# Linear attention and two MLPs on one core: k and v loaded on 112 partitions plus 16, slopes loaded later, sixteen subtractions moved to GpSimd

## The chip, the core and the metric

The kernel runs on one core of a Trainium2 chip. A core has five engines that run in parallel, each with its own list of instructions in a fixed order: TensorE (PE, matrix products), VectorE (DVE), ScalarE (ACT), GpSimd (POOL) and SyncE (SP, which here only issues transfers). A transfer (DMA) is issued by an engine's queue and carried by 16 DMA engines. Engines wait for each other and for transfers through semaphores; an instruction that waits holds up everything behind it on its engine. The metric is the device time of one execution in microseconds (us); lower is better.

## The reference

```python
def _attn_ref(q, k, v):                    # 8 batches, 8 heads, 576 tokens, 64 wide
    q_s = softmax of q over its 64 columns
    k_s = softmax of k over the 576 tokens (axis=2)
    kv = np.einsum('bhsd,bhse->bhde', k_s, v)
    return np.einsum('bhsd,bhde->bhse', q_s, kv)

x = attention, laid out as 4608 tokens x 512
x = square(relu(x @ moe_w_in)) @ moe_w_out             # MLP 1, 512 -> 2048 -> 512
h = x @ moe2_w_in                                      # MLP 2
out = (max(h, 0) + alpha * min(h, 0)) @ moe2_w_out     # alpha: one slope per hidden column
```

In the reference the softmaxes are written out (maximum, exponential, sum plus 1e-9, division), and all is float32. The weights and alpha reach the kernel as 64-bit floats, whose two words it joins into one float32 itself.

## The kernel before

**Products.** Each float32 factor is held as two fp32r parts, a head (the rounded value) and a rest (value minus head), and each product is three matrix products. For MLP 1's first matrix, `Weights` makes 16 chunks f = 0 to 15, each 128 hidden columns wide: SP loads a chunk of 64-bit words into one of two `raw` buffers (L353), ACT corrects the exponent (a rebias) (L366), DVE joins the words in two integer steps (L346, L347) into one of four `bits` buffers, ACT rounds the head (L386), and DVE subtracts it (`rest`, L389).

**Stages.** The 4608 tokens are nine tiles of 512. In the first stage each tile goes through attention and then through the 16 chunks (one unit of 12 products each, L741, evacuated by ACT in L769 and L772 and stored to DRAM). In tile 0 the first four chunks are made in 16 blocks of three products, in the order of the four x parts (L721: x part 0 with chunks 0 to 3, x part 1 with chunks 0 to 3, and so on). Later stages (MLP 1's second matrix, L781; MLP 2, L865 and L781) use sums of blocks made from tokens and weights; none of their lines is touched.

**Attention.** `sums(i, j)` makes the 64 x 64 matrices of two heads of batch i: loads k (L538), takes a maximum over the five tokens of each partition (L548, DVE), turns it on PE and takes the maximum over partitions (L553, L556, L559), subtracts it (L563, DVE), exponential (L568, ACT), product with v (L575, PE), then kv (L580 to L589). v is loaded in rows (L538 too) and copied by ACT beside columns of ones (`v_place`, L545). There are two buffers for raw k and two for raw v. `rows(i, j)` loads q (L619), softmaxes it (L625 to L645: DVE, POOL, ACT, DVE, POOL), turns it (L649), splits it (L652, L655) and multiplies it with kv (L663 to L665); the result is split into x (L668, L671).

**A load of k or v.** The 576 tokens lie five to a partition: 115 partitions of five tokens by SP's queue, and partition 115 with one token by ACT's queue (L542). 32 loads of k and 32 of v are made that way.

**Order.** All instructions are written out by a planner (`Plan.run`), which knows a cost and a due time for each operation and appends them engine by engine; so numbers in the code (costs, `due`) decide the order that each engine's list has. `due` of the rows of tile t is counted back from the tile's products by `TILE` = 40 us. The framework adds the semaphore waits. Transfers of SP and ACT use eight completion counters in turn (DMAHW0 to DMAHW7), and a transfer waits until the one eight places before it has landed.

Of the kernel before, what the change touches and what calls it, by code (L numbers as in the profile page):

```python
# [75 lines left out]
class Plan:  # L76
# [97 lines left out]
    def run(self, real):  # L174
# [8 lines left out]
        while left:  # L183
            best = None
            for engine, ops in ready.items():
                can = []
                places = {}
                for at, op in ops:
                    start = max(at, clock[engine], locked if op.lock else 0.0)
                    where = []  # L190
                    for b in op.new:
                        k = b.kind
                        if k.line[k.made + sum(1 for w in where if w[0].kind is k)] is not b:
                            break
# [24 lines left out]
            if op.engine == "sp":  # L219
                clock["sp"] = start + ISSUE  # L220
                landed = max(landed, start + 0.5) + op.mb / RATE
                op.end = max(landed, start) + LANDED - 0.5
            else:
                clock[op.engine] = op.end = start + op.cost
                if op.lock:
                    locked = op.end
            for b in op.use:
                b.left -= 1
                b.end = max(b.end, op.end)
                if not b.left:  # L230
# [11 lines left out]
def linear_attention_two_mlps(  # L242
# [20 lines left out]
    T = NT // TOK  # L263
    R = TOK // P
    KR = 5
    KP = -(-S // KR)
    VW = D + 1
    assert S - (KP - 1) * KR == 1

    const = ctx.enter_context(tc.tile_pool(name="const", bufs=1))  # L270
    psum = ctx.enter_context(tc.tile_pool(name="psum", bufs=1, space=PSUM))
# [53 lines left out]
    )  # L325

    def first():
        for kt in K["k"].homes:
            nc.vector.memset(sbuf(KR * 2 * D)(kt)[96:KP], -3.4e38)
        for vt in K["vr"].homes:  # L330
            nc.vector.memset(sbuf(KR * 2 * D)(vt)[96:KP], 0.0)
        for vt in K["v"].homes:
            nc.vector.memset(sbuf(KR * 2 * VW, KP)(vt).rearrange("p (r h w) -> p r h w", r=KR, h=2)[:, :, :, D:VW], 1.0)
        for w in K["kvw"].homes:
            nc.gpsimd.memset(sr[:, w * GRAIN:w * GRAIN + 2 * P].bitcast(F32), 0.0)
        make_identity(nc, ident)
# [39 lines left out]
    class Weights:  # L376


        def __init__(self, kd, w):
            self.bufs, self.done = [], []  # L380
            for f in range(NF):
# [3 lines left out]
                def head(bits=bits, parts=parts):  # L385
                    nc.scalar.copy(parts.ap[:, :BANK], bits.ap)  # L386

                def rest(bits=bits, parts=parts):
                    nc.vector.tensor_tensor(parts.ap[:, BANK:], bits.ap, parts.ap[:, :BANK].bitcast(F32), op=ALU.subtract)  # L389

                o = plan.add(head, "act", 0.62, [o], new=[parts], use=[bits])
                o = plan.add(rest, "dve", 0.7, [o], use=[bits, parts], lock=True)
                self.bufs.append(parts)
                self.done.append(o)

# [129 lines left out]

    def sums(i, j, after):

        kt = buf(K["k"], lambda g: sbuf(KR * 2 * D, KP)(g).rearrange("p (h r d) -> p h r d", h=2, r=KR))
        vr = buf(K["vr"], lambda g: sbuf(KR * 2 * D, KP)(g).rearrange("p (h r d) -> p h r d", h=2, r=KR))
        vt = buf(K["v"], lambda g: sbuf(KR * 2 * VW, KP)(g).rearrange("p (r h w) -> p r h w", r=KR, h=2))  # L530
        km, m, rs = buf(K["km"], sbuf(2 * D, KP)), buf(K["m"], sbuf(1)), buf(K["rs"], sbuf(1))
        ke = buf(K["ke"], sbuf(2 * KR * D, KP))
        kvw = buf(K["kvw"], lambda g: sr[:, g * GRAIN:g * GRAIN + 2 * P].rearrange("p (n m) -> p n m", n=2))
        p1, p2, p3 = bank(K["m1"]), bank(K["m2"]), bank(K["s"])
        h, last = slice(2 * j, 2 * j + 2), S - 1

        def load(to, x):
            nc.sync.dma_start(  # L538
                to.ap[:KP - 1].rearrange("p h r d -> p h (r d)"),
                x[i, h, :last, :].rearrange("h (p r) d -> p h (r d)", r=KR),  # L540
            )
            nc.scalar.dma_start(to.ap[KP - 1:KP, :, 0, :], x[i, h, last, :].unsqueeze(0))  # L542

        def v_place():
            nc.scalar.copy(vt.ap[:, :, :, :D], vr.ap.rearrange("p h r d -> p r h d"))  # L545
# [4 lines left out]
            )  # L550

        def k_max_t():
            nc.tensor.transpose(p1.ap[:, :KP], km.ap, ident[:KP, :KP])  # L553

        def k_max_all():
            nc.vector.tensor_reduce(m.ap, p1.ap[:, :KP], axis=AX.X, op=ALU.max)  # L556

        def k_max_back():
            nc.tensor.transpose(p2.ap[:KP, :P], m.ap.to_broadcast([P, KP]), ident)  # L559

        def k_shift():
# [434 lines left out]
```

## Time and profile before

| what | value |
|---|---|
| median of 3 runs | 1659.41 us (1656.95 to 1662.28) |
| the profiled execution | 1665.62 us, its span 1663.7 us |
| PE busy | 1590.5 us (96%) |
| DVE, ACT, POOL busy | 1231.4 (74%), 964.0 (58%), 254.5 (15%) |
| transfers | 287.20 MB, mean 173 GB/s |

The span runs from the first instruction to the last; the profiled execution's own time has 1.9 us more around it. PE is busy nearly all the time from 62 us to the end, so what the kernel loses lies in the time in which PE waits. A row of a timeline reads: start, duration, engine, line, operation, output <- input, how many, and in brackets the idle time before it with what ended it. "SPq" and "ACTq" are the engines' queues, in which transfers are issued.

### The profile page before, as it was taken

The numbers are of one execution on the slowest core, as the hardware profiler recorded it, in microseconds if no ns is written. First come the engines' busy times: TensorE is split into PE (matmuls) and PEld (weight loads), VectorE is DVE, ScalarE is ACT, GpSimd is POOL, SyncE is SP. The second block draws the span as 40 slices with busy tenths as digits, with TensorE's granted clock in tenths as the row PEclk, the third lists the DMA queues.
The fourth block names the chain that finished last, engine by engine and source line by source line (L and its number), as shares of the span: only waits on it lengthen the run. The fifth ranks groups of instructions, "written<-read, shape, count | busy, mean of one in ns | idle before, by whom it ended". The sixth has DMA issues, their size and how long they took to land.

```text
span 1663.7 us, 30317 instructions
## 1 busy us (share of the span) xinstructions
PE 1590.5 (96%) x11840; PEld 1491.7 (90%) x11840; DVE 1231.4 (74%) x2125; ACT 964.0 (58%) x1499; POOL 254.5 (15%) x228
## 2 busy tenths in 40 slices
PE   2789999999999999999999999999999999999998
PEld 1567888788888999999999999999999899999998
DVE  4775666666643888888878877777776998888875
ACT  2577666676756644444445677777778644444442
POOL 2111111111200000000012333333333000000012
PEclk9999999999999999999999999999999999999999
DMA  4466777778677644444446433333336644444441
GB/s 131 141 213 227 248 264 265 259 280 271 230 259 260 206 140 140 131 130 128 131 138 206 153 129 129 133 124 133 129 127 217 221 146 140 133 128 128 137 136 63
DMA packets 122112, 287.20 MB, mean 173 GB/s; under 512 B 11504, under 2 KB 70256, under 8 KB 121968
## 3 DMA queue, kind: packets, MB, share of 16 engines
q1 hardware_dynamic: 121712, 285.22, 51.4%
q8 instruction: 93, 1.52, 0.4%
q14 instruction: 51, 0.42, 0.1%
q10 hardware_dynamic: 256, 0.03, 0.0%
HBM read 168.83 MB, written 116.39 MB: 171 GB/s over the span
## 4 chain that ended last, share of the span: by engine, by line
PE 71%; DVE 10%; DMA 5%; ACT 4%; issue 3%; POOL 2%; SPq 0%; DVEq 0%; ACTq 0%; POOLq 0%
PE bank L781 41%; PE bank L741 17%; PE bank L865 10%; DVE sr L473 3%; DMA sb<-in_k_dram 1%; POOL sb L930 1%; ACT sb L914 1%; ACT sb L909 1%; DVE sb L894 1%; DMA sb<-in_moe_w_in_dram 1%; DVE sb L900 1%; PE bank L575 1%; DVE sb L489 1%; DMA sb<-in_q_dram 1%; DVE sb L917 1%
## 5 line engine op out<-in xcount | busy, mean ns | idle before, releaser
L781 PE MATMUL bank<-sr 128*128 128x256 f32 x6048 | 730.1, 283 | 5.2 <-DVE sr L473 4.4
L781 PEld LDWEIGHTS bank<-sr 128*128 128x128 f32 x6048 | 727.0, 192 | 8.3 <-DVE sr L473 7.4
L470 ACT CAST sr<-sb 128x512 fp32r<-128x512 f32 (+2 forms) x534 | 366.3, 713 | 383.7 <-PE bank L781 256.1
L473 DVE TENSOR_TENSOR sr<-sb,sr 128x512 fp32r<-128x512 f32 (+2 forms) x534 | 423.3, 817 | 121.7 <-ACT sr L470 121.1
L741 PE MATMUL bank<-sr 128*128 128x512 f32 x1680 | 408.9, 398 | 4.9 <-DVE sr L389 4.9
L741 PEld LDWEIGHTS bank<-sr 128*128 128x128 f32 x1680 | 312.7, 190 | 71.5 <-DVE sr L389 5.9
L865 PE MATMUL bank<-sr 128*128 128x256 f32 x3024 | 367.6, 284 | 8.1 <-DVE sr L473 7.3
L865 PEld LDWEIGHTS bank<-sr 128*128 128x128 f32 x3024 | 365.0, 193 | 10.5 <-DVE sr L473 9.6
L769 ACT ACTIVATE sb<-bank 128x512 f32<-128x512 f32 x144 | 85.7, 596 | 75.9 <-PE bank L741 59.8
L495 POOL TENSOR_TENSOR sb<-sb 128x256 f32<-128x256 f32 x16 | 16.5, 1034 | 735.6 <-DVE sb L489 697.6
L489 DVE TENSOR_TENSOR sb<-sb 128x512 f32<-128x512 f32 x162 | 114.4, 707 | 10.5 <-DMA sb<-y_scratch 10.1
L930 POOL TENSOR_TENSOR sb<-sb 128x1024 f32<-128x1024 f32 x36 | 89.1, 2475 | 154.5 <-ACT sb L929 118.3
L909 ACT ACTIVATE sb<-sb 128x1024 f32<-128x1024 f32 x72 | 76.3, 1059 | 44.9 <-DVE sb L906 44.2
L914 ACT ACTIVATE sb<-sb,al_neg 128x512 f32<-128x512 f32 x144 | 96.4, 716 | 2.3
L772 ACT ACTIVATE sb<-sb 128x512 f32<-128x512 f32 x144 | 90.7, 631 | 4.0 <-DMA r<-sb 0.6
L817 DVE TENSOR_TENSOR sb<-sb,bank 128x512 f32<-128x512 f32 x108 | 71.4, 684 | 21.1 <-PE bank L781 16.7
L645 POOL TENSOR_TENSOR sb<-sb 128x512 f32<-128x512 f32 x36 | 38.8, 1079 | 279.4 <-DVE sb L641 186.7
L495 DVE TENSOR_TENSOR sb<-sb 128x256 f32<-128x256 f32 x146 | 78.0, 539 | 0.5
L894 DVE TENSOR_TENSOR sb<-bank,sb 128x512 f32<-128x512 f32 x72 | 49.3, 684 | 35.8 <-ACT sb L919 23.0
L548 DVE TENSOR_REDUCE sb<-sb 116x128 f32<-116x640 f32 x32 | 41.7, 1302 | 45.0 <-DMA sb<-in_k_dram 30.6
L900 DVE TENSOR_TENSOR sb<-bank,sb 128x512 f32<-128x512 f32 x72 | 49.8, 692 | 28.3 <-PE bank L865 23.3
L903 POOL TENSOR_TENSOR sb<-sb 128x256 f32<-128x256 f32 x72 | 53.2, 740 | 106.7 <-DVE sb L894 77.2
(64 smaller groups left out, 1066.7 us busy)
## 6 DMA issues: line engine op xcount, KB each, us to landing
r<-sb SPq DMA_DIRECT2D x144, 512.0 KB
sb<-r SPq DMA_DIRECT2D x144, 512.0 KB
j<-sb SPq DMA_DIRECT2D x24, 896.0 KB
sb<-j SPq DMA_DIRECT2D x24, 896.0 KB
sb<-in_moe_w_in_dram SPq DMA_DIRECT2D x32, 512.0 KB
sb<-in_moe_w_out_dram SPq DMA_DIRECT2D x32, 512.0 KB
y_scratch<-sb SPq DMA_DIRECT2D x36, 256.0 KB
sb<-y_scratch SPq DMA_DIRECT2D x18, 512.0 KB
```

The source lines that it names most:

```text
L470: nc.scalar.copy(parts.ap[:, :n], what())
L473: nc.vector.tensor_tensor(parts.ap[:, n:], what(), parts.ap[:, :n].bitcast(F32), op=ALU.subtract)
L489: nc.vector.tensor_tensor(two(block(4, 2)), two(block(1, 2)), block(0).unsqueeze(1).to_broadcast([P, 2, HALF]), op=ALU.subtract)
L495: e.tensor_tensor(block(6), block(2), block(4), op=ALU.add)
L741: nc.tensor.matmul(h.ap, w[:, a, c, :], x_parts(x[c][0])[:, b, :], start=(c == 0 and n == 0), stop=(c == KB - 1 and n == 2),)
L769: o = plan.add(lambda: nc.scalar.activation(u.ap, h.ap, AF.Relu), "act", 0.6, [o], new=[u], use=[h])
L772: lambda: nc.scalar.activation(ro.ap[:, half], u.ap, AF.Square), "act", 0.63, [o, even], new=new, use=[u, ro]
L781: nc.tensor.matmul(target[:, m * HALF:(m + 1) * HALF], one[:, u, ms], two[:, w, :], start=start and m == 0 and i == 0, stop=stop and m == ...
L865: nc.tensor.matmul(h.ap[:, m * HALF:(m + 1) * HALF], a[:, u, c * P:(c + 1) * P], b[:, w, :], start=(m == 0 and c == 0 and z == 0), stop=(( ...
L909: nc.scalar.activation(zt.ap, block(0, 4), AF.Relu, scale=-1.0)
L914: nc.scalar.mul(half, half, al_neg[:, f:f + 1])
L930: o = plan.add(lambda: nc.gpsimd.tensor_tensor(block(0, 4), block(0, 4), zt.ap, op=ALU.add), "pool", 2.3, [o], use=[z, zt])
```

## The change

1. **k and v.** 112 partitions hold five tokens, the 16 others one. Both transfers of a load are issued by SP; ACT issues none. All tiles of `sums` now have 128 partitions. The 16 partitions' four unused places keep the values that `first` puts there (very negative for k, zero for v). The planner counts two issues for such a load.
2. **Start.** `first` runs one exponential on a column of `al` before anything else on ACT; the zeros of raw v are set by POOL instead of DVE.
3. **Rests.** The rest of a chunk f < 16, which is all of them, is made by POOL, with 1.4 us in the plan instead of 0.7.
4. **Slopes.** The load of alpha waits for tile 1's first unit, and counts 0.2 MB in the plan instead of 0.05.
5. **Due times.** The rows of tile 1 are due by 30 us per tile instead of 40.

```diff
+AT_START = 16
+TILE1 = 30.0
...
-                clock["sp"] = start + ISSUE
+                clock["sp"] = start + op.cost
...
-    KP = -(-S // KR)
+    KF = (S - P) // (KR - 1)
...
+        nc.vector.memset(al[:, :1], 0.0)
+        nc.scalar.activation(al_neg[:, :1], al[:, :1], AF.Exp)
         for kt in K["k"].homes:
-            nc.vector.memset(sbuf(KR * 2 * D)(kt)[96:KP], -3.4e38)
+            nc.vector.memset(sbuf(KR * 2 * D)(kt)[96:], -3.4e38)
         for vt in K["vr"].homes:
-            nc.vector.memset(sbuf(KR * 2 * D)(vt)[96:KP], 0.0)
+            nc.gpsimd.memset(sbuf(KR * 2 * D)(vt)[96:], 0.0)
...
-                def rest(bits=bits, parts=parts):
-                    nc.vector.tensor_tensor(parts.ap[:, BANK:], bits.ap, parts.ap[:, :BANK].bitcast(F32), op=ALU.subtract)
+                pool = f < AT_START
+
+                def rest(bits=bits, parts=parts, e=nc.gpsimd if pool else nc.vector):
+                    e.tensor_tensor(parts.ap[:, BANK:], bits.ap, parts.ap[:, :BANK].bitcast(F32), op=ALU.subtract)
...
-                o = plan.add(rest, "dve", 0.7, [o], use=[bits, parts], lock=True)
+                o = plan.add(rest, *(("pool", 1.4) if pool else ("dve", 0.7)), [o], use=[bits, parts], lock=True)
...
             nc.sync.dma_start(
-                to.ap[:KP - 1].rearrange("p h r d -> p h (r d)"),
-                x[i, h, :last, :].rearrange("h (p r) d -> p h (r d)", r=KR),
+                to.ap[:KF].rearrange("p h r d -> p h (r d)"),
+                x[i, h, :KF * KR, :].rearrange("h (p r) d -> p h (r d)", r=KR),
             )
-            nc.scalar.dma_start(to.ap[KP - 1:KP, :, 0, :], x[i, h, last, :].unsqueeze(0))
+            nc.sync.dma_start(to.ap[KF:, :, 0, :], x[i, h, KF * KR:, :].rearrange("h p d -> p h d"))
...
-        lk = plan.add(lambda: load(kt, k), "sp", ISSUE, [after], new=[kt], mb=0.295)
+        lk = plan.add(lambda: load(kt, k), "sp", 2 * ISSUE, [after], new=[kt], mb=0.295)
...
-            due = now[0] - TILE * (1 - (j + 1) / KB) - EARLY if t else LEAD + 4 * j
+            due = now[0] - (TILE if t > 1 else TILE1) * (1 - (j + 1) / KB) - EARLY if t else LEAD + 4 * j
...
-    o = plan.add(alphas, "sp", ISSUE, due=60.0, mb=0.05)
+    o = plan.add(alphas, "sp", ISSUE, [h1[1, 0]], due=60.0, mb=0.2)
```

What that does to the order is shown at three places. Line numbers of the changed kernel are four to six higher (L538 and L542 are there L544 and L548, L353 is L357, L389 is L395).

SP's list from the start of the program, before; in brackets the semaphores that an instruction waits for (DVE_49, Pool_49 and so on stand for an engine, DMAHW for the counter of a transfer):

```order
L538 DMA sb<-in_k_dram 115x2x320 [waits DVE_49]
L619 DMA sb<-in_q_dram 128x2x256
L538 DMA sb<-in_k_dram 115x2x320 [waits DVE_49]
L619 DMA sb<-in_q_dram 128x2x256
L538 DMA sb<-in_v_dram 115x2x320 [waits DMAHW0_49,DVE_49]
L538 DMA sb<-in_v_dram 115x2x320 [waits DMAHW1_49,DVE_49]
L353 DMA sb<-in_moe_w_in_dram 128x4x256 [waits DMAHW2_49]
L353 DMA sb<-in_moe_w_in_dram 128x4x256 [waits DMAHW3_49]
L956 DMA al<-in_moe_alpha_dram 128x16x1 [waits DMAHW5_49]
L538 DMA sb<-in_v_dram 115x2x320 [waits DMAHW6_49,DMAHW0_49,Activation_49]
```

The same place of the change:

```order
L544 DMA sb<-in_k_dram 112x2x320 [waits DVE_49]
L548 DMA sb<-in_k_dram 16x2x64
...
L544 DMA sb<-in_v_dram 112x2x320 [waits Pool_49]
L548 DMA sb<-in_v_dram 16x2x64
L544 DMA sb<-in_v_dram 112x2x320 [waits DMAHW0_49,Pool_49]
L548 DMA sb<-in_v_dram 16x2x64 [waits DMAHW1_49]
L357 DMA sb<-in_moe_w_in_dram 128x4x256 [waits DMAHW2_49]
L357 DMA sb<-in_moe_w_in_dram 128x4x256 [waits DMAHW3_49]
L544 DMA sb<-in_v_dram 112x2x320 [waits DMAHW6_49,DMAHW4_49,Activation_49]
```

The first load of v waits for no counter there, the load of alpha is gone from this place, and the third load of v stands right behind the two chunks of weights.

ACT's list from the start, before (L545 copies v, L634 is the exponential of q, L366 the rebias of a chunk, L568 the exponential of k):

```order
L542 DMA sb<-in_k_dram 1x2x64 [waits DVE_49] x2
L542 DMA sb<-in_v_dram 1x2x64 [waits DVE_49] x2
L545 ACT_TABLE_LOAD [waits DMAHW4_49,DMAHW0_49]
L545 COPY sb<-sb 116x10x64 [waits DVE_49]
L542 DMA sb<-in_v_dram 1x2x64 [waits Activation_49]
L545 COPY sb<-sb 116x10x64 [waits DMAHW6_49,DMAHW1_49,DVE_49]
L542 DMA sb<-in_v_dram 1x2x64 [waits DMAHW7_49,Activation_49]
L634 ACTIVATE sb<-sb 128x2x4x64 [waits DMAHW3_49,Pool_49]
L366 ACTIVATE sb<-sb 128x512 [waits DMAHW2_49]
```

And of the change:

```order
L331 ACT_TABLE_LOAD
L331 ACTIVATE al_neg<-al 128x1 [waits DVE_49]
L551 COPY sb<-sb 128x10x64 [waits DMAHW6_49,DMAHW7_49,DVE_49,Pool_49]
L551 COPY sb<-sb 128x10x64 [waits DMAHW0_49,DMAHW1_49,DVE_49,Pool_49]
L640 ACTIVATE sb<-sb 128x2x4x64 [waits DMAHW2_49,Pool_49]
L370 ACTIVATE sb<-sb 128x512 [waits DMAHW2_49]
L574 ACTIVATE sb<-sb 128x640 [waits DVE_49]
```

The table load no longer stands behind a wait for v, and no transfer stands between the computing instructions.

POOL's list of the change, behind its first four operations for q (L637 and L651 subtract the maximum from q and divide it by the sum; L395 is the rest of a chunk):

```order
L637 TENSOR_TENSOR sb<-sb 128x512 x2
L651 TENSOR_TENSOR sb<-sb 128x512
L395 TENSOR_TENSOR sr<-sb,sr 128x512 x2
L651 TENSOR_TENSOR sb<-sb 128x512
L395 TENSOR_TENSOR sr<-sb,sr 128x512 x2
L637 TENSOR_TENSOR sb<-sb 128x512
```

Before, POOL had there only the operations for q, and the rests stood in DVE's list (the second and third of them together, behind the two integer steps of both chunks and behind the sum of q in L639 to L641).

## Rows read from the trace of the kernel before

**Rows 1.** Stretches: us, busy of each engine, PE clock, DMA share, GB/s

```profile
2.90:36.50 33.60, 5.22 (x34) 3.73 (x34) 12.00 (x25) 9.93 (x16) 7.05 (x10) 1.00 0.56 155
36.50:62.80 26.30, 15.45 (x90) 10.36 (x91) 20.98 (x45) 10.34 (x19) 4.80 (x4) 1.00 0.51 144
62.80:126.00 63.20, 55.96 (x317) 44.37 (x316) 47.75 (x94) 46.21 (x85) 9.63 (x8) 0.97 0.58 182
126.00:475.00 349.00, 344.18 (x2008) 281.72 (x2007) 223.14 (x496) 238.89 (x426) 56.13 (x54) 0.99 0.74 256
```

**Rows 2.** Short stretches with transfers of one kind

```profile
34.00:35.00 1.00, 0.00 (x0) 0.00 (x0) 0.00 (x0) 0.15 (x1) 0.00 (x0) 1.00 0.33 124
48.50:50.00 1.50, 1.50 (x3) 0.83 (x3) 1.43 (x4) 1.35 (x2) 0.22 (x1) 1.00 1.09 323
```

**Rows 3.** Timeline of SP's queue, 0 to 40 us

```profile
1.55 0.39 SPq L538 DMA_DIRECT2D sb<-in_k_dram  x1
...
7.45 0.77 SPq L538 DMA_DIRECT2D sb<-in_v_dram  x2
...
10.83 2.05 SPq L956 DMA_DIRECT2D al<-in_moe_alpha_dram  x1
16.70 3.67 SPq L538 DMA_DIRECT2D sb<-in_v_dram  x2
...
27.33 0.26 SPq L538 DMA_DIRECT2D sb<-in_k_dram  x1
...
38.46 0.27 SPq L538 DMA_DIRECT2D sb<-in_k_dram  x1
```

**Rows 4.** Timeline of the computing engines, 0 to 126 us

```profile
7.46 1.23 DVE L548 TENSOR_REDUCE sb<-sb 116x128 f32<-116x640 f32 x1 [3.75 <-DMA sb<-in_k_dram]
14.65 1.28 ACT L545 ACT_TABLE_LOAD   x1 [14.65 <-DMA sb<-in_v_dram]
15.95 0.73 ACT L545 COPY sb<-sb 116x640 f32<-116x640 f32 x1
...
36.47 1.23 DVE L548 TENSOR_REDUCE sb<-sb 116x128 f32<-116x640 f32 x1 [3.40 <-issue]
43.42 1.23 DVE L548 TENSOR_REDUCE sb<-sb 116x128 f32<-116x640 f32 x1 [1.77 <-DMA sb<-in_k_dram]
50.22 2.01 PE L721 MATMUL bank<-sr 128*128 128x512 f32 x3
...
62.80 0.85 PE L721 MATMUL bank<-sr 128*128 128x512 f32 x3
...
123.04 8.23 PE L741 MATMUL bank<-sr 128*128 128x512 f32 x35 [1.58 <-DVE sr L389]
```

**Rows 5.** PE's waits, 0 to 126 us: total, times, longest

```profile
PE bank L721 <- DVE sr L389: 5.4, 1, 5.4
PE bank L741 <- DVE sr L389: 4.9, 4, 2.2
```

**Rows 6.** Lines: L389, and POOL's groups with mean ns

```profile
L389 DVE TENSOR_TENSOR sr<-sb,sr x16: 637/691/1530, 49.5 to 122.3; 128x512 fp32r<-128x512 f32 x16
L903 POOL TENSOR_TENSOR sb<-sb 128x256 f32<-128x256 f32 x72 | 53.2, 740 | 106.7 <-DVE sb L894 77.2 <-DMA y_scratch<-sb 25.6 <-DMA r<-sb 4.0
L930 POOL TENSOR_TENSOR sb<-sb 128x1024 f32<-128x1024 f32 x36 | 89.1, 2475 | 154.5 <-ACT sb L929 118.3 <-DVE sb L489 36.2
L495 POOL TENSOR_TENSOR sb<-sb x16: 732/904/1456, 852.7 to 1639.2; 128x256 f32<-128x256 f32 x16
L542 ACTq DMA_DIRECT2D sb<-in_k_dram x32: 565/566/1192, 1.6 to 417.8; - x32
```

**Rows 7.** Timeline, 93 to 95 us: POOL beside an integer step of DVE

```profile
93.20 1.04 POOL L631 TENSOR_TENSOR sb<-sb 128x512 f32<-128x512 f32 x1
93.55 0.97 DVE L346 TENSOR_SCALAR sb<-sb 128x512 int32<-128x512 int32 x1 [0.62 <-ACT sb L366]
```

**Rows 8.** L346 in all, ns lowest/median/highest

```profile
L346 DVE TENSOR_SCALAR sb<-sb x64: 407/421/972, 41.0 to 500.0; 128x512 int32<-128x512 int32 x64
```

More of the change, by code (lines that the diff above doesn't have):

```diff
@@ L265, in linear_attention_two_mlps @@
     KR = 5
-    KP = -(-S // KR)
+    KF = (S - P) // (KR - 1)
     VW = D + 1
-    assert S - (KP - 1) * KR == 1
+    assert KF * KR + P - KF == S and KF >= 96
     const = ctx.enter_context(tc.tile_pool(name="const", bufs=1))
@@ L327, in first @@
     def first():
+        nc.vector.memset(al[:, :1], 0.0)
+        nc.scalar.activation(al_neg[:, :1], al[:, :1], AF.Exp)
         for kt in K["k"].homes:
-            nc.vector.memset(sbuf(KR * 2 * D)(kt)[96:KP], -3.4e38)
+            nc.vector.memset(sbuf(KR * 2 * D)(kt)[96:], -3.4e38)
         for vt in K["vr"].homes:
-            nc.vector.memset(sbuf(KR * 2 * D)(vt)[96:KP], 0.0)
+            nc.gpsimd.memset(sbuf(KR * 2 * D)(vt)[96:], 0.0)
         for vt in K["v"].homes:
-            nc.vector.memset(sbuf(KR * 2 * VW, KP)(vt).rearrange("p (r h w) -> p r h w", r=KR, h=2)[:, :, :, D:VW], 1.0)
+            nc.vector.memset(sbuf(KR * 2 * VW)(vt).rearrange("p (r h w) -> p r h w", r=KR, h=2)[:, :, :, D:VW], 1.0)
         for w in K["kvw"].homes:
@@ L526, in sums @@
     def sums(i, j, after):
[L528 to L532, printed above, removed]
+        kt = buf(K["k"], lambda g: sbuf(KR * 2 * D)(g).rearrange("p (h r d) -> p h r d", h=2, r=KR))
+        vr = buf(K["vr"], lambda g: sbuf(KR * 2 * D)(g).rearrange("p (h r d) -> p h r d", h=2, r=KR))
+        vt = buf(K["v"], lambda g: sbuf(KR * 2 * VW)(g).rearrange("p (r h w) -> p r h w", r=KR, h=2))
+        km, m, rs = buf(K["km"], sbuf(2 * D)), buf(K["m"], sbuf(1)), buf(K["rs"], sbuf(1))
+        ke = buf(K["ke"], sbuf(2 * KR * D))
         kvw = buf(K["kvw"], lambda g: sr[:, g * GRAIN:g * GRAIN + 2 * P].rearrange("p (n m) -> p n m", n=2))
         p1, p2, p3 = bank(K["m1"]), bank(K["m2"]), bank(K["s"])
-        h, last = slice(2 * j, 2 * j + 2), S - 1
+        h = slice(2 * j, 2 * j + 2)
         def load(to, x):
             nc.sync.dma_start(
-                to.ap[:KP - 1].rearrange("p h r d -> p h (r d)"),
-                x[i, h, :last, :].rearrange("h (p r) d -> p h (r d)", r=KR),
+                to.ap[:KF].rearrange("p h r d -> p h (r d)"),
+                x[i, h, :KF * KR, :].rearrange("h (p r) d -> p h (r d)", r=KR),
             )
-            nc.scalar.dma_start(to.ap[KP - 1:KP, :, 0, :], x[i, h, last, :].unsqueeze(0))
+            nc.sync.dma_start(to.ap[KF:, :, 0, :], x[i, h, KF * KR:, :].rearrange("h p d -> p h d"))
         def v_place():
@@ L552, in k_max_t @@
         def k_max_t():
-            nc.tensor.transpose(p1.ap[:, :KP], km.ap, ident[:KP, :KP])
+            nc.tensor.transpose(p1.ap[:, :P], km.ap, ident)
         def k_max_all():
-            nc.vector.tensor_reduce(m.ap, p1.ap[:, :KP], axis=AX.X, op=ALU.max)
+            nc.vector.tensor_reduce(m.ap, p1.ap[:, :P], axis=AX.X, op=ALU.max)
         def k_max_back():
-            nc.tensor.transpose(p2.ap[:KP, :P], m.ap.to_broadcast([P, KP]), ident)
+            nc.tensor.transpose(p2.ap[:, :P], m.ap.to_broadcast([P, P]), ident)
         def k_shift():
-            t = p2.ap[:KP, :P].rearrange("p (h d) -> p h d", h=2).unsqueeze(2).to_broadcast([KP, 2, KR, D])
+            t = p2.ap[:, :P].rearrange("p (h d) -> p h d", h=2).unsqueeze(2).to_broadcast([P, 2, KR, D])
             nc.vector.tensor_tensor(
@@ L592, in kv_rest @@
                 )
-        lk = plan.add(lambda: load(kt, k), "sp", ISSUE, [after], new=[kt], mb=0.295)
+        lk = plan.add(lambda: load(kt, k), "sp", 2 * ISSUE, [after], new=[kt], mb=0.295)
         o = plan.add(k_max, "dve", 1.3, [lk], new=[km], use=[kt])
-        lv = plan.add(lambda: load(vr, v), "sp", ISSUE, [after], new=[vr], mb=0.295)
+        lv = plan.add(lambda: load(vr, v), "sp", 2 * ISSUE, [after], new=[vr], mb=0.295)
         lv = plan.add(v_place, "act", 0.75, [lv], new=[vt], use=[vr])
```

## The prediction

> **What bounds the kernel now.** PE is busy for 96% of the span, so I looked first for the stretches in which it is not, and cut the start at the events that carry it [rows 1]: a load of k, the fourth early block of products, the end of tile 0. Up to 36.5 us PE is busy for 5.2 us and no engine reaches 40%, so something outside the engines sets the pace. From 36.5 to 62.8 us PE has 15.5 of 26.3 us. From 62.8 to 126.0 us it has 56.0 of 63.2 us; tile 0's last unit starts at 123.04 us [rows 4] and takes about 3 us, so 126.0 us is tile 0's end. From 126 to 475 us, the rest of the first stage, it loses only 4.8 of 349 us. So whatever brings tile 0's end forward shortens the span by about as much, if the stages behind it keep their pace, and nothing else can give much.
>
> What paces the first stretch is the transfer of k and v. In a stretch in which only such loads are under way, the 16 DMA engines have a mean share of 0.33 and move 124 GB/s; where weights move, the share is full and the rate 323 GB/s [rows 2]. A third of 16 is five, and 115 partitions are five groups of 23: a load of 115 x 2 x 320 x 4 = 294,400 bytes runs on about five engines for 294.4/124 = 2.4 us. A load sent alone at 38.46 us is used at 43.42 us [rows 3, 4]: 4.96 us, 2.4 of moving and 2.55 around it. Nine loads of k and v come before the one used at 36.47 us: 9 x 2.4 = 21.4 us. On the same five engines lie also four loads of q (262,144 bytes at 323 GB/s, 0.8 each) and two of weights (1.6 each): 27.8 us in all, out of the 33.6 us of that stretch. The rest of the story is order: the first load of v is issued only at 7.45 us, ACT sits until 14.65 us for it, loads its table for 1.28 us, and copies at 15.95 us; the third and fourth load of v, which wait for these copies, are issued from 16.70 us [rows 3, 4].
>
> **The change part by part.** I follow one chain and write for each link when it comes now and when it should come.
>
> *k and v.* 112 partitions are seven times 16. If the load spreads like the weights do, it takes 286,720 bytes at 323 GB/s = 0.9 us; at the rate per engine of [rows 2] (124/5 = 25 GB/s) it would be 0.7. I take 0.8, so a lone load takes 0.8 + 2.55 = 3.35 us instead of 4.96. The second transfer of 16 rows costs SP one more issue, 64 in all. SP's issues that stand alone take 0.26 to 0.39 us [rows 3], and SP is idle for most of its time, so I cost them at 0.35 us where a chain runs through one and at nothing elsewhere; without that cover it would be 64 x 0.35 = 22 us. ACT is freed of its 64 issues of 0.57 us [rows 6], and of the waits that stand before them.
>
> *First k.* Issued at 1.55 us, used at 7.46 us [rows 3, 4]; that is 0.95 us more than a lone load takes, which I keep as the cost of being first. After: 1.6 + 3.35 + 0.95 = 5.9 us.
>
> *First v.* It no longer waits for a counter, and has k, q, k, q ahead of it: 1.6 + 5 x 0.8 + 2.55 + 0.95 = 9.1 us. The table is loaded during that time, so the copy starts at 9.1 us instead of 15.95 us: 6.9 us ahead. The load of alpha, 2.05 us on SP's queue [rows 3], lies behind ACT's copies now and would lie inside this lead; moved to tile 1 it is covered by SP's idle time. Left where it was it would have cost 2 us at most. The zeros for v, now POOL's, and the exponential in front fall into the 4 us in which no load has landed yet; I cost them at nothing, and at 1.3 us, a table load, if they did not fit.
>
> *Fourth k.* It is used at 36.47 us now [rows 4], 9.1 us after its issue at 27.33 us, because the loads ahead hold the five engines. After: ACT goes on from 9.1 us with two copies, two exponentials of q, one of k and a rebias; at the copy's 0.73 us each [rows 4] that is 4.4 us. Then DVE has a sum and a subtraction before k's buffer is free; as an estimate I give each the 1.23 us of the maximum [rows 4], so 16.0 us. A load takes 3.35 us: 19.4 us. That is 17.1 us ahead. The transfers before it are now 9 x 0.8 + 4 x 0.8 + 2 x 1.6 = 13.6 us, and no longer in the way.
>
> *First block of products.* From the fourth k to the first block it takes 50.22 - 36.47 = 13.75 us now, 1.77 of them a wait for the fifth k, 0.69 the rest on DVE [rows 4, 6]. Both go (the fifth k now stands behind this in DVE's list): 11.3 us, so 30.7 us, 19.5 us ahead.
>
> *Rests on POOL.* POOL's subtraction takes 0.74 us for 256 columns and 2.48 us for 1024 [rows 6], so about 0.74 + 256 x 1.735/768 = 1.3 us for 512, against 0.69 on DVE. Each chunk is 0.6 us later by that, and DVE has 16 x 0.69 = 11 us less. POOL has 16 x 1.3 = 21 us more, of which it has plenty. From the first to the fourth block it takes 12.6 us now, 5.4 of them a wait for the second rest [rows 4, 5], which stood in DVE's list behind the work for q. After, the second rest follows the first on POOL, and chunks 2 and 3 decide: their loads start when the integer steps of chunks 0 and 1 free the buffers, which stand a little past the middle of those 11.3 us in DVE's list: near 26 us (estimate). The second lands 1.6 + 1.6 + 2.55 = 5.75 us later. Then come a rebias, two integer steps, the head and the rest: one step 0.42 [rows 8], the other three at the 0.69 of a subtraction of the same 512 columns [rows 6], the rest 1.3, in all 3.8 us. That is 35.5 us without any queueing. The other bound is the present 12.6 us and 2 us for dearer rests: 45 us. I take 38, nearer to the lower since the 5.4 us have gone, and 24.8 us ahead.
>
> *From the fourth block to tile 0's end.* PE needs 56.0 us, and takes 63.2 [rows 1]. DVE waits and work shrink there, but POOL's rests come 0.6 us later and tile 1's rows are made later in the plan. Bounds: 56 (no wait is left) and 70 (some 7 us of new waits). I take 62.5: 100.5 us instead of 126.0.
>
> *Sum.* 126.0 - 100.5 = 25.5 us, of which 19.5 come before the first block, 5.3 from the first four chunks and 0.7 later. After tile 0 I take no change, within 2 us either way. Against the profiled execution's 1665.6 us that is 1640 us; that execution lies 6.2 us above the median, and I carry the difference over: 1659.4 - 25.5 = 1634 us.
>
> **A rule about two engines.** While POOL worked from 93.20 us for 1.04 us, DVE's first integer step took 0.97 us instead of the median 0.42 [rows 7, 8], so DVE was held until POOL's end. The Trainium skill, "SBUF — State Buffer", section "Who interferes with whom", says that a VectorE instruction with two SBUF inputs, or in a two-port mode, and a GpSimd instruction that reads SBUF shut each other out for a whole instruction, and that the one that comes first wins. The trace agrees, and by that rule the rests on POOL could cost DVE what they save it.
>
> **The rivals.**
> *The pace passes to ACT or to order (smaller gain).* ACT is busy for 46.2 of 63.2 us in the dense stretch [rows 1] and loses its issues, but all its work for tile 0 must fit a shorter time; tile 1's first rows are due up to 7.5 us later (a quarter to three quarters of 10 us). If that adds 7 to 15 us of waits, the gain is 10 to 18 us: 1641 to 1649 us. For it: in-order lists rarely come down to their sum. Against: PE's waits there are mostly the rests, 4.9 us [rows 5].
> *Everything goes through (larger gain).* Fourth block at 35.5 us and PE never waiting: 35.5 + 56 = 91.5 us, gain 34.5, 1625 us. For that every list must flow at once.
> *112 partitions do not spread.* Then only ACT's and SP's order at the start gives: v copied 1.28 + 2 us earlier, and the second rest; gain 3 to 8 us, 1651 to 1656 us. Against it: loads of 128 partitions reach a full share [rows 2], and 112 is a multiple of 16 as 128 is. The Trainium skill, "DMA: Bandwidth & Descriptors", section "Why a DMA increments its semaphore by 16 and not by 1", has a load run on the largest number up to 16 that divides its outermost size: five for 115, 16 for 112. The trace agrees for 115 with its 0.33; for 112 alone no stretch shows it.
> *Slower: POOL and DVE shut each other out.* A rest beside DVE's work can take up to twice as long (L495: 0.73 to 1.46 us [rows 6]), 2.6 us, and hold each of the two integer steps for up to 1.3 us. That is 1.9 + 2.6 = 4.5 us a chunk. If it falls on the path for the 12 chunks behind the first four, it is 54 us: 1634 + 54 = 1688 us. It decides from 25.5/12 = 2.1 us a chunk. Against: a rest overlaps with PE's 3 us per unit, and a hold needs both engines to meet every time.
>
> **How the numbers follow.** Forecast, a gain of 18 to 32 us: 0.57. Smaller, 8 to 18: 0.23. Larger: 0.10. No spread: 0.05. Slower: 0.03. No gain that can be told: 0.02. The predicted time is the likeliest case's, 1634 us, its own range 1627 to 1641. For 8 in 10 I leave out the largest gains beyond 33 us and those under 9 us: 1626 to 1650 us. About 0.3%, 5 us, is what a measurement of this kernel can tell from no change: faster 0.94 (the first three cases and most of the fourth), same 0.03, slower 0.03.
>
> **What would show it.** The share of the DMA engines in a stretch of k or v alone near 0.9 instead of 0.33; the first copy of v near 9 us; the fourth maximum of k near 19 us; the first block near 30 and the fourth near 38 us; POOL's rest near 1.3 us, and DVE's first integer step at a median near 0.42; tile 0's end near 100 us; PE's loss from there on as before. It would be wrong if a new wait opened between 38 and 100 us (for a head on ACT, a rest on POOL, or tile 1's x), or if tile 1 to 8 lost more than 7 us.

## The result, and the profile after

The changed kernel takes 1634.92 us (median of 4 runs, 1633.89 to 1635.94) against 1658.39 us (4 runs, 1656.95 to 1662.28) for the kernel before: a ratio of 0.9855 with a 95% interval of 0.9835 to 0.9874, 23.5 us less. The profiled execution took 1633.89 us. A second profile of the kernel before, taken for the experiments, has a span of 1658.0 us, 5.7 us less than the one shown ahead, and is the fairer one to subtract from.

The page of the kernel after, its first part: busy time, share of the span and instructions of each engine.

```profile
PE 1583.5 (97%) x11840; PEld 1487.5 (91%) x11840; DVE 1223.2 (75%) x2108; ACT 962.0 (59%) x1500; POOL 275.7 (17%) x246
```

The shares hardly moved; nearly all of POOL's 21 us more are the rests. The stretches that answer to [rows 1 and 2], cut at the same events (the load of k, the fourth early block, tile 0's end), show where the time went. Columns as there; a DMA share a little above 1 is read as full:

```profile
26.00:26.60 0.60, 0.60 (x2) 0.00 (x0) 0.57 (x3) 0.00 (x0) 0.28 (x1) 1.00 0.93 313
2.90:21.90 19.00, 5.00 (x33) 3.63 (x34) 10.90 (x20) 7.66 (x13) 8.32 (x15) 1.00 1.00 269
21.90:39.00 17.10, 13.63 (x92) 9.41 (x91) 15.47 (x36) 12.02 (x23) 7.66 (x6) 1.00 0.64 181
39.00:104.60 65.60, 57.31 (x321) 45.31 (x320) 50.45 (x95) 47.18 (x85) 27.57 (x23) 0.95 0.67 203
104.60:452.00 347.40, 347.40 (x2042) 285.77 (x2042) 224.95 (x503) 239.54 (x430) 54.95 (x53) 1.00 0.79 263
62.00:67.10 5.10, 0.82 (x3) 0.41 (x4) 4.43 (x11) 3.94 (x9) 3.27 (x3) 0.79 0.90 302
67.10:70.50 3.40, 3.40 (x8) 2.72 (x9) 3.23 (x8) 3.34 (x7) 1.38 (x2) 0.50 1.12 292
```

In the first of them only a load of k and one of v are under way: share 0.93 where [rows 2] had 0.33, 313 GB/s where it had 124. The stretch up to the fourth k is 19.0 us instead of 33.6, and the DMA engines are full in it. The next is 17.1 instead of 26.3 us. The dense one is longer, 65.6 instead of 63.2 us. Behind tile 0 PE loses nothing in 347.4 us, where it lost 4.8 in 349 [rows 1]. (The first stage itself ends later than those stretches, at 516.4 us here and at 547.4 us before; PE loses nothing in the remainder of either.)

The timeline of the computing engines after, which answers to [rows 4 and 7] (L554 is the maximum of k, L551 the copy of v, L727 an early block, L747 a unit, L559 and L565 turn maxima of k, L395 the rest, L350 and L351 the two integer steps). One row is of SP's queue, the load of k at 55.86 us:

```profile
0.73 1.28 ACT L331 ACT_TABLE_LOAD   x1 [0.73 <-PEq L985]
5.06 1.23 DVE L554 TENSOR_REDUCE sb<-sb 128x128 f32<-128x640 f32 x1 [2.58 <-DMA sb<-in_k_dram]
10.38 1.60 ACT L551 COPY sb<-sb 128x640 f32<-128x640 f32 x2 [8.15 <-DMA sb<-in_v_dram]
21.93 1.25 DVE L554 TENSOR_REDUCE sb<-sb 128x128 f32<-128x640 f32 x1 [0.91 <-DMA sb<-in_k_dram]
32.17 2.62 PE L727 MATMUL bank<-sr 128*128 128x512 f32 x6
38.90 2.21 PE L727 MATMUL bank<-sr 128*128 128x512 f32 x9
53.28 1.28 POOL L395 TENSOR_TENSOR sr<-sb,sr 128x512 fp32r<-128x512 f32 x1 [2.83 <-ACT sr L390]
53.40 1.71 DVE L351 SCALAR_TENSOR_TENSOR sb<-sb 128x512 int32<-128x512 int32 x1
55.86 0.33 SPq L544 DMA_DIRECT2D sb<-in_k_dram  x1
58.05 0.42 DVE L350 TENSOR_SCALAR sb<-sb 128x512 int32<-128x512 int32 x1
61.17 1.27 DVE L554 TENSOR_REDUCE sb<-sb 128x128 f32<-128x640 f32 x1 [2.11 <-PE bank L581]
62.37 0.68 DVE L351 SCALAR_TENSOR_TENSOR sb<-sb 128x512 int32<-128x512 int32 x1
62.59 0.30 PE L559 MATMUL bank<-ident,sb 128*128 128x128 f32 x1 [0.79 <-DVE sb L554]
63.78 2.04 POOL L637 TENSOR_TENSOR sb<-sb 128x512 f32<-128x512 f32 x2 [4.41 <-DVE sb L631]
64.49 0.52 PE L565 MATMUL bank<-ident,sb 128*128 128x128 f32 x2 [1.60 <-DVE sb L562]
65.78 1.27 POOL L395 TENSOR_TENSOR sr<-sb,sr 128x512 fp32r<-128x512 f32 x1
67.10 5.17 PE L747 MATMUL bank<-sr 128*128 128x512 f32 x12 [2.09 <-POOL sr L395]
72.94 3.04 PE L747 MATMUL bank<-sr 128*128 128x512 f32 x12
101.75 3.51 PE L747 MATMUL bank<-sr 128*128 128x512 f32 x14 [1.22 <-POOL sr L395]
```

The first copy of v starts at 10.38 us (15.95 before), the fourth k is used at 21.93 (36.47), the first block starts at 32.17 (50.22), the fourth at 38.90 (62.80), tile 0's last unit at 101.75 (123.04). Of the 23.9 us by which the fourth block is ahead, 2.6 are lost again until that unit. The rows from 62.59 to 67.10 us show where: PE waits three times within 5 us (for the maximum of k, for the maximum over partitions, for a rest that stands on POOL behind two subtractions of q), and the 12 products of the unit behind it take 5.17 instead of 3.04 us. In 67.10 to 70.50 the granted clock is 0.50 (1.2 of 2.4 GHz); in the 5.1 us ahead PE had been busy for 0.8 us. The kernel before has such a unit as well, later in tile 0, behind a wait of 2.24 us; the granted clock from 98.70 to 102.00 us is 0.54 there:

```profile
98.71 4.61 PE L741 MATMUL bank<-sr 128*128 128x512 f32 x12 [2.24 <-DVE sr L389]
```

PE's waits in the first 130 us after, as in [rows 5]:

```profile
PE bank L747 <- POOL sr L395: 5.6, 5, 2.1
PE bank L727 <- POOL sr L395: 1.4, 1, 1.4
```

The two groups of waits for a rest are still there, 7.0 us instead of 10.3. The long one ahead of the early blocks fell from 5.4 to 1.4 us; the units' is no shorter.

### The profile page after: what moved, and what is told of

Its sections match the earlier page's. It is cut to its first block, busy times and chain, and to the rows that moved or that the text cites. A ratio compares the mean times of both kernels' runs of the same rounds, so it can differ in the third digit from the quotient of the medians.

```text
span 1632.1 us, 30290 instructions
## 1 busy us (share of the span) xinstructions
PE 1583.5 (97%) x11840; PEld 1487.5 (91%) x11840; DVE 1223.2 (75%) x2108; ACT 962.0 (59%) x1500; POOL 275.7 (17%) x246
## 4 chain that ended last, share of the span: by engine, by line
PE 78%; DVE 9%; ACT 3%; issue 3%; POOL 2%; DMA 1%; DVEq 0%; SPq 0%; ACTq 0%
PE bank L787 42%; PE bank L747 22%; PE bank L871 10%; DVE sr L479 3%; POOL sb L936 1%; PE bank L581 1%; ACT sb L920 1%; ACT sb L915 1%; DVE sb L900 1%; PE bank L655 1%; DVE sb L906 1%; DVE sb L495 1%; DVE sb L923 1%; DVE sb L504 1%; ACT sb L935 1%
## 5 line engine op out<-in xcount | busy, mean ns | idle before, releaser
L747 PE MATMUL bank<-sr 128*128 128x512 f32 x1680 | 405.0, 396 | 5.6 <-POOL sr L395 5.6
L747 PEld LDWEIGHTS bank<-sr 128*128 128x128 f32 x1680 | 311.2, 189 | 71.7 <-POOL sr L395 6.9
L651 POOL TENSOR_TENSOR sb<-sb 128x512 f32<-128x512 f32 x36 | 37.8, 1052 | 244.0 <-DVE sb L647 201.7
L501 DVE TENSOR_TENSOR sb<-sb 128x256 f32<-128x256 f32 x146 | 78.1, 539 | 0.4
L504 DVE TENSOR_TENSOR sb<-sb 128x256 f32<-128x256 f32 x146 | 63.9, 438 | 4.0
```

Of the source, the lines that this page charges most:

```text
L501: e.tensor_tensor(block(6), block(2), block(4), op=ALU.add)
L747: nc.tensor.matmul(h.ap, w[:, a, c, :], x_parts(x[c][0])[:, b, :], start=(c == 0 and n == 0), stop=(c == KB - 1 and n == 2),)
```

## The experiments

Twelve kernels were run, two of them the kernels before and after again, in three groups that each shared runs of the kernel before. Ratios are to the kernel before of the same group, with 95% intervals. Events are the starts read in each kernel's trace: the fourth maximum of k, the fourth early block, the first unit behind tile 0's last rest, and the end of the first stage's last unit (us).

| kernel | median us | ratio (interval) | 4th k | 4th block | last rest used | stage 1 end | span |
|---|---|---|---|---|---|---|---|
| before, shown ahead | 1659.41 | 1 | 36.5 | 62.8 | 123.0 | 547.4 | 1663.7 |
| before, again | 1659.96 | 1.0002 (0.9989 to 1.0015) | 35.5 | 62.0 | 122.7 | 544.0 | 1658.0 |
| after | 1634.92 | 0.9855 (0.9835 to 0.9874) | 21.9 | 38.9 | 101.7 | 516.4 | 1632.1 |
| after, again | 1635.60 | 0.9852 (0.9837 to 0.9867) | 23.6 | 40.7 | 102.1 | 516.7 | 1633.9 |
| k/v on 115 and 1 | 1657.07 | 0.9974 (0.9961 to 0.9986) | 34.1 | 53.5 | 119.4 | 536.2 | 1652.9 |
| k/v alone | 1638.10 | 0.9861 (0.9846 to 0.9877) | 24.5 | 49.9 | 108.4 | 524.0 | 1639.3 |
| rests on DVE | 1643.76 | 0.9893 (0.9879 to 0.9907) | 21.8 | 42.3 | 108.8 | 524.2 | 1641.9 |
| k/v and rests alone | 1636.75 | 0.9866 (0.9846 to 0.9887) | 23.9 | 44.5 | 100.6 | 515.4 | 1634.1 |
| rests on DVE, tile 1 due by 40 | 1638.37 | 0.9881 (0.9862 to 0.9899) | 23.1 | 48.2 | 107.5 | 520.9 | 1634.9 |
| 8 rests on POOL | 1632.56 | 0.9838 (0.9819 to 0.9857) | 23.0 | 39.7 | 99.6 | 516.1 | 1631.1 |
| tile 1 due by 40 | 1635.42 | 0.9858 (0.9842 to 0.9873) | 22.5 | 43.5 | 106.0 | 519.0 | 1633.3 |
| slopes as before | 1631.91 | 0.9834 (0.9813 to 0.9854) | 24.4 | 40.9 | 99.8 | 515.2 | 1632.7 |
| one-token rows by ACT | 1633.35 | 0.9830 (0.9815 to 0.9845) | 21.1 | 38.5 | 103.5 | 518.1 | 1632.6 |
| weights behind the third k | 1635.40 | 0.9854 (0.9839 to 0.9869) | 26.5 | 40.4 | 101.9 | 516.5 | 1633.7 |

Profiles of one kernel differ by up to 6 us at the end (the first two rows), so verdicts go by the ratios, and the events say where.

### Is it the spread of the transfer?

The theory: 112 partitions run on all 16 DMA engines, and that is the gain. The rival: the order at the start gives it. Two kernels from opposite sides: the change with a load on 115 partitions and one, everything else kept; and the kernel before with the k/v part alone.

```diff
-    KF = (S - P) // (KR - 1)
+    KF = S // KR
...
-            nc.sync.dma_start(to.ap[KF:, :, 0, :], x[i, h, KF * KR:, :].rearrange("h p d -> p h d"))
+            nc.sync.dma_start(to.ap[KF:KF + 1, :, 0, :], x[i, h, KF * KR, :].unsqueeze(0))
```

> The changed kernel with the same order on every engine, but 115 partitions of five tokens and one of one token, both still by SP. Transfers are the cause: five engines carry k and v again, the share in a stretch of them alone is 0.33, and 14 to 20 us of the gain are lost (1649 to 1655 us). Order and ACT's freed issues are the cause: within 4 us of the changed kernel (1631 to 1639 us).

It keeps 0.26% of the change's 1.45%: about 20 of 24 us hang on the two numbers 112 and 16. In its trace a stretch with loads of k and v alone, and the stretch up to the fourth k:

```profile
32.00:33.50 1.50, 0.00 (x0) 0.00 (x0) 0.00 (x0) 0.69 (x2) 0.00 (x0) 1.00 0.33 121
2.90:34.10 31.20, 5.53 (x34) 3.75 (x34) 10.81 (x21) 8.49 (x15) 8.32 (x15) 1.00 0.54 167
```

And its timeline at the start:

```profile
7.16 2.09 SPq L548 DMA_DIRECT2D sb<-in_v_dram  x1
...
14.11 0.73 ACT L551 COPY sb<-sb 128x640 f32<-128x640 f32 x1 [11.88 <-DMA sb<-in_v_dram]
...
34.08 1.23 DVE L554 TENSOR_REDUCE sb<-sb 128x128 f32<-128x640 f32 x1 [3.94 <-DMA sb<-in_k_dram]
```

The share is 0.33 again and the fourth k is used at 34.08 us, though the table is loaded at 0.73 us and SP's order is the change's. The one-token issues also hold SP longer there, up to 2.09 us against 0.46 in the first 40 us of the change; how much that adds to the 12 us by which the fourth k is later, this run does not separate. The Trainium skill, "DMA: Bandwidth & Descriptors", section "Why a DMA increments its semaphore by 16 and not by 1", has a load use the largest number of engines, up to 16, that divides the slowest dimension of both its sides. The trace agrees: 0.33 for 115 and 0.93 for 112.

The other side, the kernel before with KF, the tiles of 128 partitions, both transfers on SP and the plan's count of two issues, and nothing else of the change:

```diff
-    KP = -(-S // KR)
+    KF = (S - P) // (KR - 1)
...
-            nc.scalar.dma_start(to.ap[KP - 1:KP, :, 0, :], x[i, h, last, :].unsqueeze(0))
+            nc.sync.dma_start(to.ap[KF:, :, 0, :], x[i, h, KF * KR:, :].rearrange("h p d -> p h d"))
...
```

> The kernel before with the k and v part alone (112 partitions of five tokens and 16 of one, both transfers by SP; the planner counts two issues). Transfers are the cause: most of the gain comes with this part alone, 16 to 22 us under before (1636 to 1642 us), the fourth maximum of k near 24 us instead of 36.5, and what is missing is the table load and alpha at the start (2 to 3 us) and the wait for the second rest. Order and rests are the cause: less than 8 us under before.

It has the whole gain within the intervals. The rival is out from both sides. PE's waits in its first 130 us:

```profile
PE bank L721 <- DVE sr L389: 5.8, 1, 5.8
PE bank L741 <- DVE sr L389: 5.0, 3, 3.1
```

The second rest stands in DVE's list there as it did [rows 5], and its fourth block is 11 us later than the change's. Yet the medians differ by no more than their intervals: 11 us at the fourth block are 7 at tile 0's last unit, and 1 in the ratios (0.9861 and 0.9855).

### What are the rests on POOL worth?

```diff
-AT_START = 16
+AT_START = 0
```

> The changed kernel with all rests on DVE again (AT_START = 0). By my sum the rests on POOL give 5 us around the first four chunks and next to nothing later: 3 to 6 us slower than the changed kernel (1638 to 1641 us). If POOL and DVE shut each other out at a price, it is as fast or faster (1630 to 1635 us).

Slower than the change, with intervals that don't meet (0.9893 from 0.9879, against 0.9855 up to 0.9874 and, the second time, 0.9852 up to 0.9867): 0.4%, 6 to 7 us. Its timeline:

```profile
37.07 1.65 PE L727 MATMUL bank<-sr 128*128 128x512 f32 x3 [2.43 <-DVE sr L395]
...
63.74 1.33 DVE L554 TENSOR_REDUCE sb<-sb 128x128 f32<-128x640 f32 x1 [1.55 <-DMA sb<-in_k_dram]
...
70.39 5.17 PE L747 MATMUL bank<-sr 128*128 128x512 f32 x12 [3.02 <-DVE sr L395]
...
108.78 12.80 PE L747 MATMUL bank<-sr 128*128 128x512 f32 x48 [2.39 <-DVE sr L395]
```

A stall of 3.02 us near 70 us, with a unit of 5.17 us behind it, is here too, so rests on POOL are not needed for it; the granted clock in the 5.1 us from 70.4 is 0.55. Next, the rests beside the k/v part alone, on the kernel before:

```diff
+AT_START = 16
...
+                pool = f < AT_START
+
+                def rest(bits=bits, parts=parts, e=nc.gpsimd if pool else nc.vector):
...
```

> The kernel before with k and v and the rests on POOL alone. So far k and v alone gave a ratio of 0.986, the whole change 0.985, and the whole change without the rests 0.989: the terms do not add up. If the rests are worth about 6 us beside k and v as well, and the other parts (start, slopes, due times) cost 5: a ratio near 0.982. If the parts share the same slack, so that k and v leave nothing for more: 0.984 to 0.987.

No gain over k/v alone that the medians show (0.9866 and 0.9861), though in the traces the last rest is used at 100.6 instead of 108.4 us. The other company, rests on DVE and tile 1's old due time with start and slopes of the change:

```diff
-AT_START = 16
-TILE1 = 30.0
+AT_START = 0
+TILE1 = 40.0
```

> The changed kernel with the rests on DVE and the rows of tile 1 due by 40 us: what is left beside k and v are the start and the later slopes. If the due times of 30 us cost the 6 us when DVE makes the rests: a ratio of 0.985 to 0.987, as k and v alone. If the start or the slopes cost them: 0.989 as the kernel with rests on DVE. By my sum the start is worth 2 to 3 us: 0.984.

Start and slopes beside k/v give nothing (0.9881; k/v alone 0.9861). The parts don't add up: rests on POOL are worth 6 to 7 us in the change and nothing that shows beside k/v alone. The reading is that each takes its gain from the same slack in front of tile 0's end; no run shows that by itself. Its plainest sign is the kernel with k/v and rests alone: its fourth block is 5.6 us behind the change's (44.5 and 38.9), its last rest is used 1.1 us ahead (100.6 and 101.7). Last, half of the rests:

```diff
-AT_START = 16
+AT_START = 8
```

> The changed kernel with the first eight rests on POOL and the last eight on DVE. PE waits for rests on POOL between 50 and 102 us (5.6 us in all). If that is POOL's longer time and its list: 1 to 3 us faster than the changed kernel (ratio 0.983). If DVE's list is what a rest saves there: 2 to 4 us slower (0.987).

With 0.9838 (0.9819 to 0.9857) it is not to be told from all sixteen, so it decides between neither.

### The small parts

Tile 1's due time:

```diff
-TILE1 = 30.0
+TILE1 = 40.0
```

> The changed kernel with the rows of tile 1 due by 40 us per tile as before (TILE1 = 40). The k and v part alone was about as fast as the whole change, so something else in it costs what the rests and the start give. If it is the later due times: 3 to 6 us faster than the changed kernel. If they help as meant, by keeping chunks ahead of tile 1's rows: 2 to 6 us slower. My own sum gave them nothing.

No difference, 0.9858 to 0.9852, so neither of the two expected effects; the sum's nothing held. The slopes' load as before:

```diff
-    o = plan.add(alphas, "sp", ISSUE, [h1[1, 0]], due=60.0, mb=0.2)
+    o = plan.add(alphas, "sp", ISSUE, due=60.0, mb=0.05)
```

> The changed kernel with the slopes loaded as early as before. Its 2048 pieces and SP's 2 us of issue stand at the start again: by my sum 0 to 2 us slower than the changed kernel (ratio 0.985 to 0.987).

Not slower; if anything 3 us faster, within the intervals. The one-token rows by ACT's queue:

```diff
-            nc.sync.dma_start(to.ap[KF:, :, 0, :], x[i, h, KF * KR:, :].rearrange("h p d -> p h d"))
+            nc.scalar.dma_start(to.ap[KF:, :, 0, :], x[i, h, KF * KR:, :].rearrange("h p d -> p h d"))
```

> The changed kernel with the 16 partitions of one token issued by ACT's queue instead of SP's. If ACT's issues (0.57 us each) and the waits that stand before them in its list count: 3 to 8 us slower than the changed kernel (1638 to 1643 us). If only the spread over the engines counts: within 2 us (1633 to 1637 us).

Not slower either, 0.9830 (0.9815 to 0.9845), if anything 4 us faster, within the intervals: in the changed kernel ACT's 64 issues cost nothing that shows.

### Do the transfers still set the pace?

From 2.9 to 21.9 us the change has a DMA share of 1.00. This kernel loads the first two chunks of weights, 1.05 MB, behind the third k (`k_loads` lists the loads of k; for that the attention of tile 0 is planned ahead of the weights):

```diff
-                _, o = joined_chunk(kd, w, f, None, bits, ...
+                _, o = joined_chunk(kd, w, f, k_loads[2] if f < 2 else None, bits, ...
...
+    x0 = x_from_attention(0)
...
```

> The changed kernel with the first two chunks of weights loaded behind the third k instead of before the third v. In the changed kernel the DMA engines are at a share of 1.00 from 2.9 to 21.9 us. If transfers still pace that stretch: the fourth maximum of k near 19 instead of 21.9 us and the kernel 1 to 3 us faster. If ACT's and DVE's lists pace it: no earlier, and the late chunks cost 0 to 3 us.

The same stretch in its trace:

```profile
2.90:21.90 19.00, 6.34 (x46) 4.35 (x48) 11.68 (x22) 6.96 (x13) 7.84 (x15) 1.00 0.84 236
```

The third k is used at 17.8 instead of 18.8 us, the fourth at 26.5 instead of 21.9, and the time is the same. The two chunks are issued there right ahead of the fifth v and the fourth k, which is issued 2.3 us later than in the change (19.78 and 17.49 us) and lands 6.4 us after that instead of 4.1. So in the change the transfers fill the first 22 us, but this kernel only moves the wait: whether the transfers or the lists pace that stretch it doesn't tell.

### The same kernels again

The kernel before and the change, unedited, for the spread of profiles.

> The kernel before again, for a second profile: in the first, tiles 1 to 8 cost 9 us more than in the changed kernel, 4.8 of them waits of PE. If the loads of k and v cause that, the second profile shows 3 to 6 us of waits between 126 us and the stage's end as well; if it was that one execution, under 1.5 us.

PE's waits from 126 to 475 us in the second profile of before:

```profile
PE bank L664 <- DVE sr L655: 2.4, 1, 2.4
PE bank L575 <- ACT sb L568: 1.6, 2, 0.8
```

The first is not a chance of one execution: the first profile has the same wait of L664, 2.3 us, at the same place (162 us). The waits of L575 lie at other places in the two profiles.

> The changed kernel again, beside the same runs of the kernel before as the next ones. First measurement: a ratio of 0.9855; it should come again within 0.003. In its second profile the fourth maximum of k, the first block and the last chunk's unit should start within 1 us of the first profile's 21.9, 32.2 and 101.8 us.

The ratio came again (0.9852) and the last chunk's unit too (102.1 us); the fourth k and the first block did not, at 23.6 and 33.8 us, each 1.6 us later than in the first profile. So events of single profiles tell no less than 2 us. Here too PE waits for nothing from tile 0's end to the end of the stage.

## Why the prediction came out

Its forecast of 1634 us was right, and so was the mechanism, the loads of k and v that spread over the engines. That the sum came within 1 us is luck in part: tile 0's end came 4 us less ahead than forecast, and the first stage behind it gained 7 to 10 us where nothing was forecast.

- **112 partitions spread.** Right, 0.93 in a stretch of k and v alone. Its rival without the spread (gain 3 to 8 us) is what the kernel on 115 partitions did: 4.3 us.
- **First k, first v.** 5.06 us (5.9 predicted) and 10.38 (9.1).
- **Fourth k.** 21.93 us, 2.5 late of 19.4. The step that failed is the sum of the transfers before it, "9 x 0.8 + 4 x 0.8 + 2 x 1.6 = 13.6 us, and no longer in the way". Nine loads of k and v (the fourth k itself among them) with their 16 rows, four of q and two of weights are 4.75 MB, so 13.6 us means 349 GB/s. The stretch ran at 269 GB/s with a full share, by which they are 17.7 us. Of the 2.5 us, 1.5 lie ahead of the issue (17.49 us, with k's buffer forecast free at 16.0; v's first copy was 1.3 us late by then), and 1.1 between issue and use (4.4 us for 3.35). That the full transfers cost both is read from the share; the kernel with the weights later does not separate them from the lists on ACT and DVE.
- **First and fourth block.** 32.17 us (30.7) and 38.90 (38); the wait for the second rest went away as forecast. From the fourth k to the first block it was 10.2 us, less than the 11.3.
- **Fourth block to tile 0's end.** Mis-sized: 62.5 us forecast, 65.6 measured. The condition "a new wait between 38 and 100 us" came true at 62 to 67 us: 4.5 us of waits, and 5.17 - 3.04 = 2.1 us for a unit at the lower clock. A slow unit is not new in itself (before has the one at 98.71 us), so these 6.6 us are not all added. Where it starts can be read in DVE's list. The unit's chunk, f = 7, has its first integer step at 58.05 us and its second only at 62.37, because the maximum of a k stands between them and DVE is idle 2.11 us ahead of it: of the load, issued from 55.86 us, the second part (issued at 56.24 us) landed 4.8 us after its issue. The profile names PE for that wait; in the second profile of the change (1.63 us) and with the rests on DVE (1.55 us, at 63.74) it names the load of k at the same place. The rest then stands on POOL behind two subtractions of q. So here a load of k still holds the chunks, through DVE's order. This is read from the traces; no kernel with that maximum elsewhere was run.
- **Tile 0's end** was 21.3 us ahead by the start of the last unit, where 25.5 were forecast.
- **After tile 0: no change, within 2 us.** Mis-sized the other way. From the last unit to the stage's end it takes 414.6 us, against 424.3 and 421.3 in the two profiles of before; 4 to 5 us of that are PE's waits that are gone. All kernels with the new tiles and plan lie at 413 to 417. Some 5 us of it are tile 1, whose last unit ends 57.7 and 58.4 us after tile 0's before, and 52.8 after; in the profile shown ahead 4 more are tile 4, with a wait of 2.0 us for an exponential of k. In tile 1 the trace of before shows what the wait of L664 comes from:

```profile
151.60 0.27 SPq L538 DMA_DIRECT2D sb<-in_k_dram  x1
158.50 1.33 DVE L548 TENSOR_REDUCE sb<-sb 116x128 f32<-116x640 f32 x1 [4.26 <-DMA sb<-in_k_dram]
161.53 0.69 DVE L655 TENSOR_TENSOR sr<-bank,sr 128x512 fp32r<-128x512 f32 x1
162.28 0.33 PE L664 MATMUL bank<-sr 128*128 128x128 f32 x1 [2.27 <-DVE sr L655]
```

DVE is idle 4.26 us for a k that is used 6.9 us after its issue, and the rest of q that PE needs (L655) stands behind that maximum in DVE's list. The slow load alone does not make the loss: with 115 partitions and the change's order DVE is idle 6.74 us for a k in tile 1 (at 140.91 us), PE waits 0.4 us there, and the stage takes 416.9 us. Nor does ACT's queue alone: with the one-token rows on ACT it is 414.6. Whether it needs both, or the old order, stays open; what the kernels without the loss share is the tiles of 128 partitions and the plan's count of two issues, which moves the order.
- **Rests on POOL, and the slower rival.** The rest takes 1.29 us in the median (1.3 predicted). DVE was held, as the rival has it: at 53.40 us the second integer step takes 1.71 instead of 0.69 us while POOL works from 53.28. But over tile 0 that is small. Of before (30 to 124 us) and of after (20 to 102 us), busy and mean ns of one:

```profile
L389 DVE TENSOR_TENSOR sr<-sb,sr 128x512 fp32r<-128x512 f32 x16 | 11.6, 731 | 1.7 <-ACT sr L386 1.4
L347 DVE SCALAR_TENSOR_TENSOR sb<-sb 128x512 int32<-128x512 int32 x16 | 11.0, 686 | 0.3
L346 DVE TENSOR_SCALAR sb<-sb 128x512 int32<-128x512 int32 x16 | 7.6, 472 | 5.9 <-ACT sb L366 5.7
```

```profile
L351 DVE SCALAR_TENSOR_TENSOR sb<-sb 128x512 int32<-128x512 int32 x16 | 11.9, 750 | 0.3
L350 DVE TENSOR_SCALAR sb<-sb 128x512 int32<-128x512 int32 x16 | 8.9, 558 | 4.7 <-ACT sb L370 4.6
```

The integer steps take 20.8 instead of 18.6 us, 2.2 us more, for 11.6 us of rests that DVE no longer does. The Trainium skill's rule ("SBUF — State Buffer", section "Who interferes with whom"), that a VectorE instruction with two SBUF inputs and a GpSimd instruction that reads SBUF shut each other out for a whole instruction, agrees with the single row; that it could eat the whole saving does not show in these two lines, and DVE's other instructions were not summed.
- **ACT's issues, alpha, due times.** Costed at nothing or at 2 us at most, and no run shows that they cost anything.

Against the second profile of before the sum is 20.9 us up to tile 0's last unit, 6.7 more up to the stage's end, and 1.7 lost behind it: 25.9 us of span, with medians 23.5 apart. Forecast were 25.5 and nothing. The 1.7 us can't be told from chance: behind the stage the two profiles of before are 2.4 us apart.

## What to carry to other kernels

Look at the DMA share in a stretch where only one kind of load moves: a third of full was here the sign of a load on a third of the engines, and a partition count that splits evenly (112 and 16 for 115 and 1) was worth about 20 of 24 us. Cost a queue of such loads by the mean rate of a long stretch, not by the peak rate of a short one, and sum bytes before saying that transfers are out of the way. When several parts of a change all bring the same event forward, their gains may share the slack: here the loads alone gave what all five parts gave. And look at what stands behind the first user of a load in its engine's list: both in tile 0 of the change and in tile 1 of before, a maximum that waited for k held work on DVE that needed no k.

## What the runs showed of the hardware

The stall of PE cost more than its own length: behind 5.1 us with 0.8 us of work, the granted clock was 0.50 for 3.4 us and a unit of 12 products took 5.17 instead of 3.04 us. In the first 40 us a one-row transfer of k or v held SP's queue for up to 2.09 us when the share of the loads was 0.33, and one of 16 rows for 0.46 us at most when it was 0.93; over the whole program the longest are 2.75 and 1.53 us. At a full DMA share the rate was anywhere between 252 GB/s (18.8 to 19.8 us of the change) and 345 GB/s (32 to 34 us), so the share alone did not give the rate.
